# A fused attention and two-layer network kernel: weight conversion later in a double step, second-layer weights fetched in quarters, the last y stores on ScalarE's queue, two pools moved

## The chip, the cores and the metric

The kernel runs on one core of a Trainium2 chip. The metric is the device time of one execution in microseconds. Before the change three runs took 1278.15, 1279.85 and 1282.69 us, median 1279.85 us.

## The reference

```
o = softmax(q k^T / 8) v            # 8 batches x 8 heads, in 9 chunks of 64 rows, head size 64
x = o as [4608 tokens, 512]
h = x @ w_in                        # 512 -> 1024
s = h * softmax(h);  z = (s - mean) / sqrt(var + 1e-6) * g_ln
y = z @ w_out                       # 1024 -> 512
h2 = y @ w_in2                      # 512 -> 2048
out = (max(h2, 0) + alpha * min(h2, 0)) @ w_out2      # 2048 -> 512
```

All inputs arrive as 64-bit floats and the result is 32-bit. Each product of the two networks is built from three matmuls on operands split into a high and a low part. The weights are converted to such pairs on the chip.

## The kernel before, in words

All instructions are issued in the order in which the program writes them. Each engine works through its own list, and waits where an operand or a buffer is not free yet.

**Phase 1** (to about 567 us) takes 36 tiles of 128 tokens through attention, the first network and its normalisation. The first ten tiles follow a written list. From tile 10 each turn of a loop, called a step here, emits the entries of STEP for step i; an entry `name+d` means operation `name` of tile i+d. The ones that matter below: `hm` (L456, L462) multiplies x by w_in; `sq` (L492) squares; `xh` and `xl` (L442, L447) split the next x; `zv` (L497) makes the variance; `pw` (L503, on GpSimd) takes its power -1/2; `zs` (L507, VectorE) scales by it; `qs` and `qn` (L395, L402, VectorE) sum and normalise the attention weights of a later tile; `tr` (L409, TensorE) transposes these, right behind `hm`.

Beside this, `conv` converts one unit of weights: ScalarE takes the top bits apart (L142, L143), VectorE makes the low part (L154 `g`, L157 `f`), GpSimd makes the sign (L148) and the sum (L342). In front of that it runs what is due for the second network's weights: sums of two blocks on GpSimd (L220), a split in high (`hi`, L229, ScalarE) and low (`lo`, L230, GpSimd), and the stores of both to DRAM. Every step has one `conv`. The steps in `twice` have a second one; such a step is called a double step here. There are three: 20, 24 and 28.

The list LAST ends phase 1: it stores the last results y (`ysb`, two stores of 128 KB each, ystore, L565 and L569) and begins phase 2's first loads.

**Phase 2** (about 567 to 926 us) computes the first product of the second network, with seven products where a plain two by two block scheme has eight. Tokens are taken in six groups of 768 (s), features in eight blocks (b): 48 units. A unit has 42 matmuls in seven products, p1, p6, p5, p7, p2, p3, p4, into four PSUM banks `hx`, `hy`, `hz`, `hv`; p2, p3 and p4 add to banks that p1, p5 and p7 filled, after the first value of the bank has been read. ScalarE and VectorE turn the banks into four results `g`, stored by SyncE as `gd` (192 KB each). There are six `g` buffers, and a buffer is written again only when its store has landed. The weights of one block, W[b], are 1792 KB. W[0] and W[1] are loaded during LAST, W[2] and W[3] behind LAST, and W[4] to W[7] one each in the units 0 to 3 (load_w, L686). In the last token group each W[b] is replaced by the output weights of the same number, behind unit b (L691).

**Phase 3** computes the last product from `gd` and these weights, with operands named `f..` and `r..`.

SBUF pools grow from a left and a right end. Phase 2's pools lie on those of phase 1, and a tile there waits until the tile of phase 1 under it has been used for the last time. From the right end the order of phase 1 is `e`, `s`, `sm`, `zt` (the tile `zz`, read by the last matmuls of phase 1), `wo1`, `y`; that of phase 2 is a small tile, then the weights W[2], W[7], W[3], W[6], W[5], W[4], then the `g` buffers.

Of the kernel before, what the change touches and what calls it, by code (L numbers as in the profile page):

```python
# [9 lines left out]
F32 = mybir.dt.float32  # L10
F32R = mybir.dt.float32r
# [19 lines left out]
YT = 4  # L31
YG = 128 * YT
YP = 256
SG = 384
NS = NT // (2 * SG)
PAIRS = NT // 2
NB2 = KF2 // 2
# [5 lines left out]
def order(text):  # L43

    return [(m[1], int(m[2])) for m in re.finditer(r"([a-zA-Z]+)([-+]?\d+)", text)]
# [23 lines left out]
STEP = order(  # L69
    """  # L70
    q+3 v+3 ye-6 zh-2 zl-2 conv+0 hm+0 tr+1 te+1 qk+2 hx+0 he+0 qm+2 qe+2 pv+1 zt-1 so+0 sq+0
    ya-5 conv+1 xh+1 xl+1 zv+0 pw+0 qs+2 zs+0 qn+2 yb-5 yx-5
    """
)
CONV = order(
    """
    p+0 l-1 s+0 a-1 f+2
# [15 lines left out]
def tile_chunk_attention_solu_prelu(  # L93
# [12 lines left out]
    nc = tc.nc  # L106
# [11 lines left out]
    y_dram = [dram.tile([128, K1, 2 * SG], F32, name=f"yd{j}") for j in range(NS)]  # L118
# [3 lines left out]
    wi_dram = dram.tile([128, NB2, 2, 7, 2, 128], F32, name="wid")  # L122
    wo_dram = dram.tile([128, NB2, 2, 7, 256], F32, name="wod")
# [44 lines left out]
    def phase1():  # L168
        with ExitStack() as c1, ExitStack() as c0:
            L = lambda name, bufs, **k: c0.enter_context(tc.tile_pool(name=name, bufs=bufs, side="left", **k))  # L170
            R = lambda name, bufs, **k: c1.enter_context(tc.tile_pool(name=name, bufs=bufs, side="right", **k))
# [6 lines left out]
            ep = R("e", 1)  # L178
            sp = R("s", 2)
            sm = R("sm", 2)  # L180
            ztp = R("zt", 1)
            wop = R("wo1", 1)
            yp = R("y", 2)
# [5 lines left out]
            qs, vs = {}, {}  # L189
# [15 lines left out]
            for kk in range(K1):  # L205
                for n in range(2):
                    c = slice(512 * n, 512 * n + 512)
# [4 lines left out]
            raws, tops, parts, his = {}, {}, {}, {}  # L212
# [117 lines left out]
            def unit_sign(u, eng):  # L330
                tops[u] = conv_sign(stage, *tops[u], eng)
# [28 lines left out]
            def unit_lo(u, eng):  # L360
                f, hi = parts.pop(u), his.pop(u)
                eng.tensor_tensor(out=units[u][2] if u < UI else wo["l"][:, u - UI], in0=f, in1=hi.bitcast(F32), op=ALU.subtract)  # L362
# [200 lines left out]
            def ystore(j, m):  # L563
                y = yp.tile([128, YG], F32, name="ysb", tag="ysb")
                nc.scalar.activation(out=y, in_=ypend.pop((j, m)), func=AF.Copy)  # L565
                pairs = (0, 1) if Z_SLOTS[j][0][0] < Z_SLOTS[j][1][0] else (1, 0)
                for c, p in enumerate(pairs):
                    g, o = divmod(j * YG + p * YP, 2 * SG)
                    nc.sync.dma_start(out=y_dram[g][:, m, o:o + YP], in_=y[:, c * YP:(c + 1) * YP])  # L569

            def yevac(s):
                assert ("yb", s) in done
# [4 lines left out]
            def yfirst(s):  # L577
# [10 lines left out]
                q=load_q, v=load_v, f=fetch, p=unit_top, l=unit_low, h=unit_hi,  # L588
                s=lambda u: unit_sign(u, nc.gpsimd), S=lambda u: unit_sign(u, nc.vector),
                a=lambda u: unit_add(u, nc.gpsimd), A=lambda u: unit_add(u, nc.vector),  # L590
                o=lambda u: unit_lo(u, nc.gpsimd), O=lambda u: unit_lo(u, nc.vector),
# [3 lines left out]
                g=lambda _: nc.sync.dma_start(out=g_sb, in_=g_ln.rearrange("(k p) -> p k", p=128)),  # L595
# [24 lines left out]
            for name, i in FIRST:  # L620
                if name in "ho" and i >= UO:
                    run_post(next(u for u in range(len(units)) if ("a", u) not in done) + 1)
                else:
                    emit(name, i)
            twice = {20, 24, 28}
            k = 0
            while ("p", k) in done:
                k += 1
            for i in range(FIRST_TILES, TILES):
                for name, d in STEP:  # L630
                    if name == "conv":
                        if d == 0 or i in twice:
                            run_post(k)
                            for c, e in CONV:
                                emit(c, k + e)
# [33 lines left out]
    def phase2():  # L669
        with ExitStack() as c2:  # L670
            def P(name, bufs, side="left", stack=c2, **k):
                return stack.enter_context(tc.tile_pool(name=name, bufs=bufs, side=side, reuse_waits="tile", **k))

            NL = 2
            wl = P("w2l", 1)
            ps2 = [P("ps_2l", 1, space=PSUM)]
            ca = c2.enter_context(ExitStack())
            tp = [P(f"t2{i}", 1, stack=ca) for i in range(26)]
            up = P("u2", 1, stack=ca)
            wr = {}  # L680
            W, raw, th, tl = {}, {}, {}, {}

            def load_w(b, src):
                W[b] = (wr.get(b) or wl).tile([128, 2, 7, 256], F32R, name=f"w2{b}", tag=f"w{b}")
                if src is wi_dram:
                    nc.sync.dma_start(  # L686
                        out=W[b].bitcast(F32).rearrange("p t i c -> p (t i c)"),
                        in_=src[:, b].rearrange("p t i k c -> p (t i k c)"),
                    )
                else:  # L690
                    nc.sync.dma_start(out=W[b].bitcast(F32), in_=src[:, b])  # L691

# [9 lines left out]
            def free(t):  # L704
                slots.append(homes.pop(t.name))

            def load_y(s):
                at[0] = s % 2 == 0
                for t in ("11", "12", "22", "21"):
                    r, c = int(t[0]) - 1, int(t[1]) - 1  # L710
                    raw[t] = slot(F32 if t == "12" else F32R, f"y{t}", at[0])
                    nc.sync.dma_start(
                        out=raw[t].bitcast(F32), in_=y_dram[s][:, 2 * r:2 * r + 2, SG * c:SG * c + SG]
                    )
# [134 lines left out]
            for b in range(NL):  # L849
                load_w(b, wi_dram)  # L850
# [12 lines left out]
                wr[b] = P(f"w2r{b}", 1, side="right")  # L863
            ps2.append(P("ps_2r", 1, side="right", space=PSUM))
            gp = P("g2", 1, side="right", stack=ca)
            for b in range(NL, NL + 2):
                load_w(b, wi_dram)

# [4 lines left out]
            src, t4s, ops, ops0 = {}, {}, {}, {}  # L875
# [154 lines left out]

            early = {(4, 1): "p1", (5, 1): "p6", (6, 1): "p5", (6, 2): "p7", (7, 1): "p2", (7, 2): "p3", (7, 3): "p4"}
            sums = {(2, 0): 0, (2, 3): 1, (3, 0): 2, (4, 0): 3}
            prev, first = None, []
            for s in range(NS):
                for b in range(NB2):
                    def extra(k):
                        if s == 0 and k == 1 and NL + 2 + b < NB2:
                            load_w(NL + 2 + b, wi_dram)
                        if s + 1 == NS:
                            if (b, k) == (0, 3):  # L1040
                                load_g(pieces[0])
                            if (b, k) == (6, 5):
                                load_g(pieces[1])
                            if b in (3, 4, 5, 6) and k in (2, 3):
                                if (b, k) == (3, 2):
                                    first.append(first_piece(pieces[0]))
                                next(first[0])
                        else:
                            if (b, k) == (1, 0):
                                load_y(s + 1)  # L1050
                            if (b, k) in sums:
                                sum_y(sums[b, k])
                            if (b, k) in early:
                                high_y(s + 1, early[b, k])
                            if (b, k - 1) in early:
                                low_y(s + 1, early[b, k - 1])

                    prev = unit(s * NB2 + b, s, b, prev, extra)
                    if s + 1 == NS and b < 7:
                        load_w(b, wo_dram)  # L1060
            for k in range(3):
                prev.late(k)
            for t, p in enumerate(GROUPS[0]):
# [27 lines left out]
    with tc.manual_schedule():  # L1091
        phase1()
# [32 lines left out]
```

## Time and profile before

| | |
|---|---|
| median of three runs | 1279.85 us |
| the profiled execution | 1281.57 us, its span 1279.7 us |
| busy share of the span | TensorE 97%, its weight loads 87%, VectorE 73%, ScalarE 53%, GpSimd 26% |
| mean granted TensorE clock | 0.990 of full speed |

TensorE has something to do nearly all the time, so time can be gained only where it waits. In the profile the time of an instruction is counted from the span's start. Behind an instruction, `[us <-X]` is the idle time of its engine in front of it and what ended it. SPq is SyncE's queue of transfers. PE is TensorE, DVE VectorE, ACT ScalarE, POOL GpSimd. In a matmul's row the time is from its start to its modelled end; neighbours overlap.

### The profile page before, as it was taken

Reading aid. Unit: us, or ns where it says so; the run is one execution under the profiler, and the core shown is the slowest. Engines: PE = TensorE matmul, PEld = TensorE weight load, DVE = VectorE, ACT = ScalarE, POOL = GpSimd, SP = SyncE. Lnnn points to the kernel's source line nnn. Section 1 sums busy time; section 2 is a strip of 40 time slices with the busy share of each in tenths; the row PEclk is TensorE's granted clock in tenths of the full one; section 3 lists DMA queues with packets and bytes.
Section 4 is the critical chain, followed back from the end, with each engine's and each line's share of the span. In section 5 each row is a group of like instructions: output and inputs, shape, how many; then the busy total and the mean of one; then the engine's idle time right before and its main releaser. Section 6 shows DMA issues by size and latency. Waiting matters only on the chain. (4 is left out here: it accounts for less than half of the span.)

```text
span 1279.7 us, 21741 instructions
## 1 busy us (share of the span) xinstructions
PE 1236.0 (97%) x8160; PEld 1108.6 (87%) x8160; DVE 933.9 (73%) x1423; ACT 682.4 (53%) x1140; POOL 326.6 (26%) x309
## 2 busy tenths in 40 slices
PE   6789999999999899998999999999999999999998
PEld 5678888888888788888999999999989888888898
DVE  6985587777877677434878787777876959678684
ACT  6685455556555555434666676665644344344442
POOL 4664155535565644412020202200000000000000
PEclk9889999999999999998999999999999999999999
DMA  8453356554656552549343443428996638374462
GB/s 323 154 150 110 104 170 186 172 183 154 229 188 229 177 180 75 201 157 380 139 157 116 151 158 114 155 111 302 338 341 207 223 119 295 97 264 148 159 220 99
DMA packets 145225, 237.88 MB, mean 186 GB/s; under 512 B 14432, under 2 KB 99936, under 8 KB 143072
## 3 DMA queue, kind: packets, MB, share of 16 engines
q1 hardware_dynamic: 144960, 235.71, 53.7%
q8 instruction: 64, 1.05, 0.3%
q0 software_dynamic: 160, 0.79, 0.1%
q14 instruction: 41, 0.34, 0.1%
HBM read 149.68 MB, written 86.77 MB: 185 GB/s over the span
## 5 line engine op out<-in xcount | busy, mean ns | idle before, releaser
L789 DVE SCALAR_TENSOR_TENSOR g<-ng,nal,g 128x384 f32<-128x384 f32 x192 | 123.7, 644 | 50.4 <-ACT g L667 50.4
L667 ACT ACTIVATE ng<-g 128x384 f32<-128x384 f32 x144 | 75.8, 526 | 128.1 <-DVE g L661 128.1
L750 PE MATMUL hx<-th,w 128*128 128x384 f32 x384 | 113.8, 337 | 5.1 <-ACT s L667 5.1
L164 PE MATMUL yps<-zz,wo_h 128*128 128x512 f32 x288 | 115.2, 400 | 0.0
L750 PE MATMUL hv<-th,w 128*128 128x384 f32 x384 | 113.6, 336 | 0.4 <-DVE g L661 0.4
L750 PE MATMUL hz<-th,w 128*128 128x384 f32 x384 | 113.7, 336 | 0.3 <-DVE wv L661 0.3
L166 PE MATMUL yps<-zz,wo_l 128*128 128x512 f32 x288 | 112.4, 390 | 0.0
L165 PE MATMUL yps<-zz,wo_h 128*128 128x512 f32 x288 | 112.2, 390 | 0.0
L983 PE MATMUL oz<-rhi,w 128*128 128x512 f32 (+1 forms) x304 | 93.8, 369 | 0.6 <-DVE osb L661 0.6
L983 PE MATMUL ox<-rhi,w 128*128 128x512 f32 (+1 forms) x304 | 93.8, 369 | 0.0
L983 PE MATMUL ov<-rhi,w 128*128 128x512 f32 (+1 forms) x304 | 93.7, 369 | 0.0
L664 POOL TENSOR_TENSOR yt<-y,y 128x384 f32<-128x384 f32 x24 | 26.9, 1140 | 240.0 <-DMA y<-yd 240.0
L667 ACT ACTIVATE rhi<-rt 128x1024 fp32r<-128x1024 f32 (+1 forms) x56 | 54.6, 984 | 61.7 <-DVE rt L664 16.3
L667 ACT ACTIVATE g<-g 128x384 f32<-128x384 f32 x144 | 75.2, 522 | 3.1
L750 PEld LDWEIGHTS hx<-th,w 128*128 128x128 f32 x384 | 71.3, 189 | 5.8 <-ACT s L667 5.8
L664 DVE TENSOR_TENSOR rlo<-rt,rhi 128x1024 fp32r<-128x1024 f32 (+1 forms) x56 | 62.5, 1126 | 15.4 <-ACT rhi L667 15.1
L750 PEld LDWEIGHTS hv<-th,w 128*128 128x128 f32 x384 | 71.3, 189 | 0.9 <-DVE g L661 0.9
L750 PEld LDWEIGHTS hz<-th,w 128*128 128x128 f32 x384 | 71.3, 189 | 0.6 <-DVE wv L661 0.6
L456 PE MATMUL h<-wi_h,xh 128*128 128x512 f32 x256 | 69.3, 393 | 0.0
L456 PE MATMUL h<-wi_l,xh 128*128 128x512 f32 x256 | 68.8, 390 | 0.2 <-POOL wi_l L362 0.2
L492 ACT ACTIVATE eh<-sl,st 128x1024 f32<-128x1024 f32 x36 | 41.5, 1152 | 45.0 <-DVE st L487 45.0
L750 PE MATMUL hx<-y,w 128*128 128x384 f32 x192 | 64.5, 336 | 0.0
(179 smaller groups left out, 3268.6 us busy)
## 6 DMA issues: line engine op xcount, KB each, us to landing
gd<-g SPq DMA_DIRECT2D x192, 192.0 KB, 1.8
qkt<-in_qk SPq DMA_DIRECT2D x36, 512.0 KB, 5.3
w<-wid SPq DMA_DIRECT2D x8, 1792.0 KB, 10.9
w<-wod SPq DMA_DIRECT2D x8, 1792.0 KB, 10.1
rc<-gd SPq DMA_DIRECT2D x24, 512.0 KB, 3.9
rd<-gd SPq DMA_DIRECT2D x24, 512.0 KB, 4.9
raw<-in_moe_w_out SPq DMA_DIRECT2D x24, 511.8 KB, 4.4
vt<-in_v SPq DMA_DIRECT2D x36, 256.0 KB, 4.4
```

The lines of the kernel that those rows point to most:

```text
L164: nc.tensor.matmul(o, lh, rh, start=first, stop=False)
L165: nc.tensor.matmul(o, lh, rl, start=False, stop=False)
L166: nc.tensor.matmul(o, ll, rh, start=False, stop=last)
L456: nc.tensor.matmul(ps[:, n], xh[:, kk], w[:, kk, 512 * n:512 * n + 512], start=(kk == 0 and w is wi_h), stop=False,)
L492: nc.scalar.activation(out=e, in_=s, func=AF.Square, bias=st[:, 4:5], accum_out=st[:, 5:6])
L664: eng.tensor_tensor(out=out, in0=a, in1=b, op=ALU.subtract)
L667: nc.scalar.activation(out=out, in_=in_, func=func, **k)
L750: nc.tensor.matmul(self.ps[x], w[:, a, i, k], d[:, k], start=(p not in CHAINED and k + j == 0), stop=(k == 1 and j == 2), skip_group_check ...
L789: nc.vector.scalar_tensor_tensor(out=self.g[t], in0=self.n[t], scalar=nal_sb[:, f:f + 1], in1=self.g[t], op0=ALU.mult, op1=ALU.add)
L983: nc.tensor.matmul(bank[key, m][:, :n], W[2 * j + k][:, a, i, 128 * m:128 * m + 128], d[:, k], start=(p not in CHAINED and j + k + q == 0) ...
```

## The change

1. The steps with a second conversion are 20, 26 and 31 in place of 20, 24 and 28. The second one now stands behind `pw`, where it stood in front of `xh`.
2. A pool of 2 KB per partition, never used, stands between `sm` and `zt`. The small phase 2 pool `u2` moves from the left end to the right, behind the `g` buffers.
3. The y stores of the last two groups of four tiles are issued by ScalarE.
4. Behind LAST only W[2] is loaded. The blocks W[3] to W[7] are loaded in four quarters of 448 KB each during the units 0 to 4, at places 0, 2, 3 and 5 of the seven places of a unit, so one block per unit and three units ahead of its use. The output weights of block b are loaded in the same way during unit b+1.
5. The four loads of the next token group's y stand at four places of unit 1 in place of one.

```diff
-    ya-5 conv+1 xh+1 xl+1 zv+0 pw+0 qs+2 zs+0 qn+2 yb-5 yx-5
+    ya-5 xh+1 xl+1 zv+0 pw+0 conv+1 qs+2 zs+0 qn+2 yb-5 yx-5
+TWICE = {20, 26, 31}
...
             sm = R("sm", 2)
+            R("pad", 1).tile([128, 512], F32, name="pad")
...
-                    nc.sync.dma_start(out=y_dram[g][:, m, o:o + YP], in_=y[:, c * YP:(c + 1) * YP])
+                    (nc.sync if j < YT + 3 else nc.scalar).dma_start(
...
-            up = P("u2", 1, stack=ca)
...
-            for b in range(NL, NL + 2):
-                load_w(b, wi_dram)
+            up = P("u2", 1, side="right", stack=ca)
+            load_w(NL, wi_dram)
...
+                c = slice(0, 3584) if q is None else slice(896 * q, 896 * q + 896)
+                nc.sync.dma_start(out=to[:, c], in_=of[:, c])
...
+            parts = (0, 2, 3, 5)
...
-                        if s == 0 and k == 1 and NL + 2 + b < NB2:
-                            load_w(NL + 2 + b, wi_dram)
+                        if s == 0 and k in parts and NL + 1 + b < NB2:
+                            load_w(NL + 1 + b, wi_dram, parts.index(k))
+                        if s + 1 == NS and b and k in parts:
+                            load_w(b - 1, wo_dram, parts.index(k))
...
-                            if (b, k) == (1, 0):
-                                load_y(s + 1)
+                            if b == 1 and k < 4:
+                                load_y(s + 1, YQ[k:k + 1])
...
-                    if s + 1 == NS and b < 7:
-                        load_w(b, wo_dram)
```

**GpSimd in step 20**, a double step before and after. `st<-st,mhalf` is `pw`; `lo`, `a` (the sign) and `f` (the sum) are the two conversions. Before:

```order
L148 TENSOR_TENSOR a_3439<-pos,neg 128x512
L342 TENSOR_TENSOR f_3436<-f_3436,a_3277 128x512
L230 TENSOR_TENSOR lo<-f_3436,hi 128x512
L230 TENSOR_TENSOR lo<-f_2953,hi 128x512
L148 TENSOR_TENSOR a_3566<-pos,neg 128x512
L342 TENSOR_TENSOR f_3563<-f_3563,a_3439 128x512
L503 TENSOR_TENSOR st<-st,mhalf 128x1
```

And with the change:

```order
L149 TENSOR_TENSOR a_3443<-pos,neg 128x512
L344 TENSOR_TENSOR f_3440<-f_3440,a_3281 128x512
L505 TENSOR_TENSOR st<-st,mhalf 128x1
L232 TENSOR_TENSOR lo<-f_3440,hi 128x512
L232 TENSOR_TENSOR lo<-f_2957,hi 128x512
L149 TENSOR_TENSOR a_3576<-pos,neg 128x512
L344 TENSOR_TENSOR f_3573<-f_3573,a_3443 128x512
```

`pw` moved ahead of the four operations of the second conversion; in the lists of ScalarE and VectorE `xh`, `xl` and `zv` moved ahead of it in the same way, and VectorE's `g` and `f` stand between `zv` and `qs`.

**SyncE's queue at the start of phase 2**, with what each transfer waits for: DMAHW0 to DMAHW7 are eight counters that the transfers use in turn, so such a wait is mostly one for the landing of the transfer eight places back. `w` is a block of weights, `yd<-ysb` a y store, `y<-yd` a y load. Before:

```order
L569 DMA yd_70<-ysb 128x256 [waits DMAHW6_49,Activation_49]
L569 DMA yd_70<-ysb 128x256 [waits DMAHW7_49]
L686 DMA w_6338<-wid 128x3584 [waits DVE_49,DMAHW0_49,PE_49,Pool_49]
L686 DMA w_6340<-wid 128x3584 [waits DMAHW1_49]
L686 DMA w_6362<-wid 128x3584 [waits DMAHW2_49]
L794 DMA gd_76<-g 128x384 [waits DMAHW3_49,DVE_49]
L794 DMA gd_73<-g 128x384 [waits DMAHW4_49,DVE_49]
L712 DMA y_6432<-yd_66 128x2x384 [waits DMAHW5_49]
```

And with the change, from W[1] (`w_6103`) on; `w_6343` is W[2], `w_6357` W[3]:

```order
L692 DMA w_6103<-wid 128x3584 [waits DMAHW3_49,DVE_49,PE_49]
L692 DMA w_6343<-wid 128x3584 [waits DVE_49,DMAHW0_49,PE_49,Activation_49]
L692 DMA w_6357<-wid 128x896 [waits DMAHW7_49,DVE_49,PE_49]
L692 DMA w_6357<-wid 128x896 [waits DMAHW2_49]
L692 DMA w_6357<-wid 128x896 [waits DMAHW3_49]
L797 DMA gd_76<-g 128x384 [waits DMAHW4_49,DVE_49]
L797 DMA gd_73<-g 128x384 [waits DMAHW5_49,DVE_49]
L692 DMA w_6357<-wid 128x896 [waits DMAHW6_49]
L692 DMA w_6438<-wid 128x896 [waits DMAHW7_49]
L715 DMA y_6440<-yd_66 128x2x384 [waits DMAHW0_49]
```

In front of the first `gd` store three whole blocks became one block, which follows W[1] directly, and three quarters.

**ScalarE at the same place**: `ysb` is the evacuation of the last y result, `s<-hx` the first of phase 2. Before:

```order
L667 ACTIVATE th<-y_6096 128x768 [waits DMAHW2_49,DMAHW0_49]
L565 ACTIVATE ysb<-yps 128x512 [waits DMAHW1_49,DMAHW0_49,PE_49]
L667 ACTIVATE th<-yt_6182 128x768
L565 ACTIVATE ysb<-yps 128x512 [waits DMAHW3_49,DMAHW2_49,PE_49]
L667 ACTIVATE s_6352<-hx 128x384 [waits PE_49]
```

And with the change:

```order
L671 ACTIVATE th<-yt_6183 128x768
L567 ACTIVATE ysb<-yps 128x512 [waits DMAHW4_49,DMAHW3_49,PE_49]
L571 DMA yd_70<-ysb 128x256 [waits DMAHW0_49,Activation_49]
L571 DMA yd_70<-ysb 128x256
L671 ACTIVATE s_6355<-hx 128x384 [waits PE_49]
```

In all sixteen stores moved into ScalarE's list, and one of the last two also waits for a counter, DMAHW0, that belongs to the transfer of W[2].

## Rows read from the trace of the kernel before

**Rows 1.** The page, part 1: TensorE's busy time, share, instructions; then other engines.

```profile
PE   1236.0 (97%) x8160; PEld 1108.6 (87%) x8160; DVE 933.9 (73%) x1423; ACT 682.4 (53%) x1140; POOL 326.6 (26%) x309
```

**Rows 2.** Timeline, the transposes `tr`: start us, us, engine, line, operation, count, [idle before].

```profile
309.40 0.60 PE L409 MATMUL et<-ident,e 128*128 128x128 f32 x4
325.20 0.63 PE L409 MATMUL et<-ident,e 128*128 128x128 f32 x4 [0.90 <-DVE e L402]
...
412.08 0.60 PE L409 MATMUL et<-ident,e 128*128 128x128 f32 x4
426.47 0.60 PE L409 MATMUL et<-ident,e 128*128 128x128 f32 x4
444.56 0.63 PE L409 MATMUL et<-ident,e 128*128 128x128 f32 x4 [3.46 <-DVE e L402]
...
460.51 0.60 PE L409 MATMUL et<-ident,e 128*128 128x128 f32 x4
```

**Rows 3.** Timeline of double step 28: `pw`, `zs`, `qn`.

```profile
440.43 0.55 POOL L503 TENSOR_TENSOR st<-st,mhalf 128x1 f32<-128x1 f32 x1
...
441.01 1.75 DVE L507 TENSOR_SCALAR sl<-sl,st 128x1024 f32<-128x1024 f32 x1 [3.86 <-POOL st L503]
...
442.68 1.74 DVE L402 TENSOR_TENSOR e<-e,r 128x512 f32<-128x512 f32 x1
```

**Rows 4.** Timeline of the regular step 31: `zs`, `qn` and the `tr` behind them.

```profile
483.38 0.76 DVE L507 TENSOR_SCALAR sl<-sl,st 128x1024 f32<-128x1024 f32 x1
...
484.06 0.69 DVE L402 TENSOR_TENSOR e<-e,r 128x512 f32<-128x512 f32 x1
...
489.30 0.60 PE L409 MATMUL et<-ident,e 128*128 128x128 f32 x4
```

**Rows 5.** Timeline, VectorE's part of a conversion while GpSimd works.

```profile
501.13 0.86 DVE L154 TENSOR_SCALAR g<-a 128x512 uint16<-128x512 uint16 x1
...
502.03 1.66 DVE L157 SCALAR_TENSOR_TENSOR f<-raw,g 128x512 f32<-128x512 uint32 x1
```

**Rows 6.** Timeline, the first matmul of p6 in units 0, 1 and 4.

```profile
568.33 0.33 PE L750 MATMUL hy<-th,w 128*128 128x384 f32 x1
...
575.61 0.33 PE L750 MATMUL hy<-th,w 128*128 128x384 f32 x1
...
606.30 0.33 PE L750 MATMUL hy<-th,w 128*128 128x384 f32 x1
```

**Rows 7.** Timeline, the weight transfers at the start of phase 2 and the stall.

```profile
569.05 1.29 SPq L686 DMA_DIRECT2D w<-wid  x3
...
587.85 0.56 DVE L661 TENSOR_TENSOR g<-hz,u 128x384 f32<-128x384 f32 x1 [6.60 <-DMA gd<-g]
...
590.39 0.69 PE L750 MATMUL hx<-th,w 128*128 128x384 f32 x1 [4.22 <-ACT s L667]
```

**Rows 8.** Windows: stretch, length, engines' busy time, granted clock, DMA share, GB/s.

```profile
10.00:12.00 2.00, 1.12 (x12) 0.91 (x8) 1.97 (x4) 1.01 (x2) 1.14 (x2) 1.00 1.03 412
...
542.00:544.00 2.00, 2.00 (x14) 1.78 (x14) 0.00 (x0) 1.06 (x2) 2.00 (x3) 1.00 1.01 430
...
558.00:560.00 2.00, 2.00 (x10) 1.66 (x9) 1.03 (x2) 1.06 (x2) 0.00 (x0) 1.00 0.38 131
```

**Rows 9.** DMA issues, 558 to 560 us: transfer, issuer, count, size, us to landing.

```profile
yd<-ysb SPq DMA_DIRECT2D x1, 128.0 KB, 1.8
```

**Rows 10.** Timeline, the last y evacuation and the first `g` of unit 0.

```profile
567.46 0.60 ACT L565 ACTIVATE ysb<-yps 128x512 f32<-128x512 f32 x1 [1.39 <-PE yps L166]
...
571.65 0.56 DVE L661 TENSOR_TENSOR g<-hv,wv 128x384 f32<-128x384 f32 x1 [0.48 <-PE hv L750]
```

**Rows 11.** Timeline, the first matmul of p6 in units 46 and 47.

```profile
912.06 0.33 PE L750 MATMUL hy<-th,w 128*128 128x384 f32 x1
...
920.06 0.33 PE L750 MATMUL hy<-th,w 128*128 128x384 f32 x1
```

**Rows 12.** Chain of work that ended last, in the same stretch: start us, us, what.

```profile
905.88 11.23 DMA gd<-g
```

More of the change, by code (lines that the diff above doesn't have):

```diff
@@ L568, in ystore @@
                     g, o = divmod(j * YG + p * YP, 2 * SG)
-                    nc.sync.dma_start(out=y_dram[g][:, m, o:o + YP], in_=y[:, c * YP:(c + 1) * YP])
+                    (nc.sync if j < YT + 3 else nc.scalar).dma_start(
+                        out=y_dram[g][:, m, o:o + YP], in_=y[:, c * YP:(c + 1) * YP]
+                    )
             def yevac(s):
@@ L624, in phase1 @@
                     emit(name, i)
-            twice = {20, 24, 28}
+            twice = TWICE
             k = 0
@@ L678, in phase2, with load_w @@
             tp = [P(f"t2{i}", 1, stack=ca) for i in range(26)]
-            up = P("u2", 1, stack=ca)
             wr = {}
             W, raw, th, tl = {}, {}, {}, {}
[L683 to L691, printed above, removed]
+            def load_w(b, src, q=None):
+                if not q:
+                    W[b] = (wr.get(b) or wl).tile([128, 2, 7, 256], F32R, name=f"w2{b}", tag=f"w{b}")
+                to = W[b].bitcast(F32).rearrange("p t i c -> p (t i c)")
+                of = src[:, b].rearrange("p t i k c -> p (t i k c)" if src is wi_dram else "p t i c -> p (t i c)")
+                c = slice(0, 3584) if q is None else slice(896 * q, 896 * q + 896)
+                nc.sync.dma_start(out=to[:, c], in_=of[:, c])
             slots = list(range(26))
@@ L705, in free, with load_y @@
                 slots.append(homes.pop(t.name))
-            def load_y(s):
+            YQ = ("11", "12", "22", "21")
+            def load_y(s, which=YQ):
                 at[0] = s % 2 == 0
-                for t in ("11", "12", "22", "21"):
+                for t in which:
                     r, c = int(t[0]) - 1, int(t[1]) - 1
```

## The prediction

> **What bounds the kernel now.** Read first the busy shares: TensorE is at work 97% of the span [rows 1], so the change can win only where TensorE waits, and the next question is where. The list of TensorE's waits names the lines, and the timeline of these lines gives the price of each, by comparing distances between equal points of the program rather than adding idle times: what follows a wait runs slower for a while too (the first matmul after the long stall takes 0.69 us instead of 0.33 [rows 7, 6]), and a distance has both.
>
> In phase 1 the transposes come every 14.39 us in regular steps (412.08 to 426.47 [rows 2]). Around step 28 the two distances are 18.09 and 15.95 us, 5.26 more than two regular ones; around step 20 one is 15.80, 1.41 more [rows 2]. That is 6.67 us lost in double steps; the third, 24, cost less and is left out. The cause: in step 28 `pw` runs only at 440.43, behind both conversions in GpSimd's list; VectorE had stood idle 3.86 us for it, then needed 1.75 and 1.74 us for `zs` and `qn` [rows 3], and the transposes waited 3.46 us [rows 2].
>
> In phase 2 a unit takes 7.28 us (568.33 to 575.61). Unit 4 should have come 29.12 us after unit 0, but came after 37.97 [rows 6]: 8.85 us lost. Three whole blocks of weights, 5.5 MB, are issued at 569.05; the first stores of results stand behind them, a result waits 6.60 us for its buffer, and TensorE 4.22 us for the bank [rows 7].
>
> At the end of phase 2 unit 47 came 8.00 us after unit 46 [rows 11], 0.72 too late, in a stretch where a store took 11.23 us to land [rows 12]. The rest of phase 3 is a row of matmuls that the change doesn't touch.
>
> **Double steps.** Nothing is added or removed: a second conversion is moved in three steps. `pw` no longer stands behind it, so it follows `zv` at once, as in a regular step. There `qn` ends at 484.75 and `tr` starts at 489.30 [rows 4]: 4.55 us to spare. What is late next is VectorE: `g` and `f` now stand between `zv` and `qs`, and GpSimd's half of the second conversion now runs beside `zs` and `qn`. Beside GpSimd `g` and `f` take 0.86 and 1.66 us [rows 5], `zs` 1.75 in place of 0.76 and `qn` 1.74 in place of 0.69 [rows 3, 4]: in all 2.52 + 0.99 + 1.05 = 4.56 us at most, just the spare time. So the stall goes, with nothing to spare; for what is handed on to the next step (its first reduction starts late) I take 0.3 us per double step, between 0 and 1.0 (the lengthening of one slowed VectorE operation). This gives 6.67 - 0.9 = 5.8 us gained, with ends of 3.7 and 7.1 (step 24 as well).
>
> The Trainium skill says why the slowed operations must be counted: "SBUF — State Buffer", section "Who interferes with whom", has VectorE and GpSimd share one pair of ports under an exclusive lock, held for a whole instruction, by operations with two inputs in SBUF too. The trace agrees: 1.74 against 0.69 us for `qn`. Without this rule one would expect three double steps free of any loss; with it they just fit.
>
> **The start of phase 2.** With the pad W[2] no longer lies on `zz`, and it follows W[1] directly in SyncE's queue, since the twelve y stores between them are gone; these two loads fall into LAST, where the transfers have room (a share of 0.38 at 558 us [rows 8]). W[3] still lies on `zz` and starts at the end of phase 1, but only three quarters of it, 1.38 MB instead of 5.5 MB, precede the first result stores. At 426 GB/s (430 at a share of 1.01 [rows 8]) that is 3.2 us, over before unit 0's first stores at about 574 us. In the 7.3 us behind, four stores, four quarters and four y loads pass, 0.79 + 1.84 + 1.57 = 4.2 MB or 9.9 us: transfers fall some 2.6 us behind. A result buffer is written again about one unit, 7.28 us, after its result is stored; 2.6 plus 1.8 for landing [rows 9] leaves 2.9 us. So the wait of 6.60 us goes. I leave 0.75 us as lost, with ends of 0 and 2.6 (if the backlog shows in full): 8.85 - 0.75 = 8.1 gained, from 6.2 to 8.85.
>
> New there: the last two y stores are issued by ScalarE in front of `s`. The trace shows no transfer issued by ScalarE; the nearest row is SyncE's, 1.29 us for three, 0.43 each [rows 7], taken whole; the other end is none. The evacuation ends at 568.06 [rows 10], so `s` starts at 568.9 and ends half a microsecond later. p2, the first product that needs it, comes three products of 1.04 us after 568.33, at 571.45: nothing waits. The first `g` now lies where the last y was and waits for its stores. Issued by 568.9 they land at 570.7, and `g` starts at 571.65 [rows 10]; even 2 us later, since they share the engines with W[3], `g` would end at 573.3, before p4 at 573.53. Price nothing; the other fourteen stores fall where ScalarE is half idle (53% busy [rows 1]). Pad and `u2` move addresses only. The loads of y at four places, in the five later token groups, come at most 3.5 us later and are needed a unit later: nothing either.
>
> **The end of phase 2.** Seven blocks of 1.835 MB now travel as quarters, with rows of 3.5 KB instead of 14 KB. The nearest row is of 512 KB loads with 4 KB rows, 412 GB/s at a share of 1.03, so 400; the whole blocks had 426, and stores with rows of 1 KB 131 at 0.38, so 345 [rows 8]. A block takes 4.31 us at 426, 4.59 at 400, 5.32 at 345: 0.28 more each, 2.0 for seven; at the far end 7.1. The transfers are the limit of this stretch, so I count it whole. Against it stands the 0.72 us of unit 47: a store now queues behind one quarter, not a block. Net loss 1.3, from a gain of 0.7 to a loss of 7.1.
>
> The Trainium skill speaks against the quarters: "DMA: Bandwidth & Descriptors", section "Bandwidth", asks for transfers of at least 1 MiB to reach 75% of the peak. The row of 512 KB loads at 400 GB/s, with several under way at once, does not bear it out; were it to hold, the loss would be like the far end's.
>
> **Sum.** -5.8 - 8.1 + 1.3 = -12.6 us. The profiled execution took 1281.57 us, 1.72 more than the median; so 1269.0 for such an execution and 1267.2 against the median 1279.85.
>
> **Rivals.**
> 1. *The double steps keep their loss.* VectorE's slowed operations use up the spare time exactly; if the next step starts late each time, or steps 26 and 31 meet GpSimd's longer conversions, the 5.8 is not gained: -6.8, 1273.0. For it: no reserve. Against: step 20 ran `pw` three conversions late and lost only 1.41.
> 2. *Quarters travel slowly.* At 345 GB/s the end loses 7.1 - 0.7 = 6.4: -7.5, 1272.4. For it: rows of 3.5 KB are shorter; against: the 4 KB rows. The skill's rule on 1 MiB would act here.
> 3. *ScalarE is held.* One of the last two y stores waits for W[2]. If W[2] still had to wait for `zz`, it would land near 567.7 + 4.3 + 1.8 = 573.8, `s` would end at 574.4, and p2 would wait 3 us, some 4.5 with the slow matmuls behind (3.46 us of waiting cost 5.26 at step 28): -8.1, 1271.8. Against: W[2] ends where the pad ends.
> 4. *Slower: eight transfers under way.* A transfer waits for the one eight places back, and with quarters a unit has just eight. So in units 41 to 47 no unit can be shorter than a transfer's way from issue to landing. With 7.28 us or less that costs nothing; at the 11.23 us of [rows 12] it is 3.95 us for each of seven units, 27.7: +13.8 (without the 1.3), 1293.7. It decides from 7.28 + 13.9 / 7 = 9.3 us on. For it: that row. Against: it stood behind a whole block, and a backlog of eight is 1.84 + 0.79 = 2.6 MB, 6.6 us at 400 GB/s.
>
> **How the numbers follow.** The forecast has 0.73, the rivals 0.10, 0.05, 0.06 and 0.06. A measurement of this kernel tells 0.3%, 3.8 us, from no change. The forecast's own range is from 1263 (all losses gone, the end even) to 1272; with the first three rivals and some allowance for two at once it reaches 1275, and below 1260, where the waits at phase 3's start would have to go too, I expect nothing. Rivals 1 to 3 are faster as well; faster 0.90, within 0.3% 0.05 (two rivals together), slower 0.05, nearly all of it rival 4.
>
> **What would show it.** Transposes every 14.4 us through steps 20, 26 and 31, with `pw` right behind `zv`. The first matmuls of p6 in units 0 to 4 at 7.28 us, no wait of a `g` for its store, W[2] issued near 543 us. ScalarE's last y stores short, with `s` less than 1 us late. In the last token group units near 7.3 us, and stores landing in under 7 us. A new TensorE wait at steps 27 or 32, or units of 8 us in the last group, would make it wrong.

## The result, and the profile after

The changed kernel takes 1267.98 us (median of 5 runs, 1267.67 to 1268.12), the kernel before 1279.80 in the runs beside it; the ratio is 0.9906, with an interval from 0.9891 to 0.9920. The prediction was 1267.2. The profiled execution of the changed kernel took 1267.81 us (span 1265.8).

**Phase 1.** The timeline around step 26, now a double one: transposes (L411), `pw` (L505), `zs` (L509), `qn` (L404), and what is left of a stall.

```profile
393.74 0.60 PE L411 MATMUL et<-ident,e 128*128 128x128 f32 x4
...
401.34 0.55 POOL L505 TENSOR_TENSOR st<-st,mhalf 128x1 f32<-128x1 f32 x1 [3.11 <-DVE st L499]
...
403.52 1.62 DVE L509 TENSOR_SCALAR sl<-sl,st 128x1024 f32<-128x1024 f32 x1
...
404.55 1.62 POOL L149 TENSOR_TENSOR a<-pos,neg 128x512 bf16<-128x512 bf16 x1
...
405.07 1.65 DVE L404 TENSOR_TENSOR e<-e,r 128x512 f32<-128x512 f32 x1
...
406.13 1.62 POOL L344 TENSOR_TENSOR f<-f,a 128x512 f32<-128x512 f32 x1
...
407.78 0.63 ACT L231 ACTIVATE hi<-f 128x512 fp32r<-128x512 f32 x1 [3.38 <-POOL f L344]
...
408.14 0.60 PE L411 MATMUL et<-ident,e 128*128 128x128 f32 x4
...
409.93 0.57 ACT L416 ACTIVATE ets<-et 128x512 f32<-128x512 f32 x1
...
410.56 1.15 PE L432 MATMUL xd<-ets,vt 64*64 64x64 f32 x32 [0.75 <-ACT ets L416]
...
423.49 0.60 PE L411 MATMUL et<-ident,e 128*128 128x128 f32 x4
```

The transpose behind the double step comes in time (14.40 us), since `pw` now waits only for VectorE's `zv`, and `qn` ends 1.42 us ahead of it; in [rows 2, 3] the transpose had to wait for `qn`. But the distance after it is 15.35. The first copy of step 27's conversion, `hi<-f`, reads a sum that GpSimd finishes at 407.75, as the last work of the second conversion of step 26; ScalarE waits 3.38 us for it, evacuates the transposes late, and `xd` waits 0.75. The same happens in step 32 (15.36); behind step 20 nothing does (14.39, 14.45). Over all steps, 5.2 us are gained of the 6.67 of [rows 2, 3].

**The end of phase 1 and the start of phase 2**, timeline: W[2], the y stores on ScalarE's queue (ACTq), and unit 0 (`hy` is the first product of p6).

```profile
535.19 0.32 SPq L692 DMA_DIRECT2D w<-wid  x1
...
536.70 0.81 ACTq L571 DMA_DIRECT2D yd<-ysb  x2
...
547.46 0.60 ACT L567 ACTIVATE ysb<-yps 128x512 f32<-128x512 f32 x1 [7.22 <-DMA yd<-ysb]
...
552.26 0.50 PE L165 MATMUL yps<-zz,wo_h 128*128 128x512 f32 x1 [0.79 <-ACT ysb L567]
...
560.75 1.27 SPq L692 DMA_DIRECT2D w<-wid  x3
...
561.39 0.81 ACTq L571 DMA_DIRECT2D yd<-ysb  x2
561.62 0.33 PE L753 MATMUL hy<-th,w 128*128 128x384 f32 x1
...
562.25 0.49 ACT L671 ACTIVATE s<-hx 128x384 f32<-128x384 f32 x1 [0.89 <-PE hx L753]
...
567.87 0.56 DVE L665 TENSOR_TENSOR g<-hv,wv 128x384 f32<-128x384 f32 x1 [3.42 <-DMA yd<-ysb]
...
568.49 0.44 PE L753 MATMUL hv<-th,w 128*128 128x384 f32 x1 [1.50 <-DVE g L665]
...
570.70 0.33 PE L753 MATMUL hy<-th,w 128*128 128x384 f32 x1
...
585.26 0.33 PE L753 MATMUL hy<-th,w 128*128 128x384 f32 x1
...
592.93 0.33 PE L753 MATMUL hy<-th,w 128*128 128x384 f32 x1
```

The waits of 6.60 and 4.22 us in [rows 7] are gone. Unit 4 comes 31.31 us after unit 0, against 37.97 in [rows 6]; the 2.19 us still lost are 1.80 in unit 0 and 0.39 in unit 3. In unit 0 the first `g` waits for the last y stores, which lie where it writes. The DMA issues show why. The last pair, 561 to 562 us:

```profile
yd<-ysb ACTq DMA_DIRECT2D x2, 128.0 KB, 5.3
```

A store that landed in 1.8 us in [rows 9] needs 5.3 (4.7 and 5.9 for the two) among three quarters of W[3], the first of them issued 0.6 us ahead on the other queue. Behind W[1] and W[2] it is worse; the first store of the pair at 536.70 (issues from 535 to 537 us):

```profile
yd<-ysb ACTq DMA_DIRECT2D x1, 128.0 KB, 9.7
```

For this pair ScalarE waits 7.22 us, and hands 0.79 to TensorE. W[1], issued at 528.48, took 13.2 us to land, until 541.65. So W[2], issued at 535.19, went out where the transfers were full (windows, columns as in [rows 8]):

```profile
535.00:541.60 6.60, 6.60 (x32) 5.44 (x31) 2.18 (x2) 2.96 (x4) 5.50 (x7) 1.00 1.00 423
541.60:547.00 5.40, 5.40 (x26) 4.46 (x24) 0.00 (x0) 0.00 (x0) 0.00 (x0) 1.00 0.92 351
```

**What a wait costs beyond itself.** The third number from the end of a windows row is TensorE's granted clock. Two stretches of the kernel before, behind its waits of 3.46 us [rows 2] and 4.22 us [rows 7], and one of the changed kernel, behind its 1.50 us in unit 0:

```profile
444.50:449.00 4.50, 4.43 (x72) 4.18 (x73) 4.43 (x7) 1.83 (x4) 2.09 (x2) 0.65 0.58 198
590.40:594.00 3.60, 3.60 (x11) 3.60 (x12) 2.08 (x4) 0.72 (x2) 2.51 (x3) 0.50 1.06 447
568.50:571.00 2.50, 2.50 (x14) 2.50 (x15) 1.35 (x3) 2.00 (x5) 0.00 (x0) 1.00 0.04 10
```

With the long waits the clock fell, from 590.40 on to 0.50 of full speed, which is 1.2 GHz in place of 2.4; behind the 1.50 us it stayed at 1.00. So removing those two waits gained more than their own length; the distances contain both.

**The end of phase 2.** Unit 47 comes 7.28 us after unit 46 (8.00 in [rows 11]):

```profile
898.69 0.33 PE L753 MATMUL hy<-th,w 128*128 128x384 f32 x1
...
905.97 0.33 PE L753 MATMUL hy<-th,w 128*128 128x384 f32 x1
```

But the first wait of the last phase is longer. TensorE's waits from 905 to 940 us (line, releaser, us in all, times, longest):

```profile
PE ox L986 <- DVE ra L668: 2.4, 1, 2.4
```

The same wait in the kernel before:

```profile
PE ox L983 <- DVE ra L664: 1.6, 1, 1.6
```

From unit 47 to the last product 355.22 us pass, 0.86 more than before.

### The profile page after: what moved, and what is told of

It reads as the page before. It is cut to its first block, busy times and chain, and to the rows that moved or that the text cites. A ratio compares the mean times of both kernels' runs of the same rounds, so it can differ in the third digit from the quotient of the medians.

```text
span 1265.8 us, 21771 instructions
## 1 busy us (share of the span) xinstructions
PE 1227.7 (97%) x8160; PEld 1102.9 (87%) x8160; DVE 935.3 (74%) x1423; ACT 682.5 (54%) x1140; POOL 327.9 (26%) x309
## 3 DMA queue, kind: packets, MB, share of 16 engines
q8 instruction: 64, 1.05, 0.3%
## 4 chain that ended last, share of the span: by engine, by line
PE 47%; DMA 5%; DVE 1%; issue 0%; SPq 0%; ACT 0%; DVEq 0%; ACTq 0%
PE oz L986 7%; PE ov L986 7%; PE ox L986 7%; PE hz L753 7%; PE hv L753 6%; PE hx L753 6%; PE oy L986 3%; PE hy L753 3%; DMA w<-wod 3%; DMA rc<-gd 1%; DMA gd<-g 0%; DVE rt L668 0%; DVE rb L668 0%; DVE rlo L668 0%; DVE u L665 0%
## 5 line engine op out<-in xcount | busy, mean ns | idle before, releaser
L167 PEld LDWEIGHTS yps<-zz,wo_l 128*128 128x128 f32 x288 | 54.0, 188 | 11.7
```

Of the source, the lines that this page charges most:

```text
L167: nc.tensor.matmul(o, ll, rh, start=False, stop=last)
```

## The experiments

Every kernel was timed in 5 rounds beside the kernel before. All distances below are read from the timelines: "steps" from the transpose near 138 us to the last of phase 1; "LAST" from there to `hy` of unit 0; "start" what ten units from unit 0 on take beyond 72.8 us; "end" from `hy` of unit 47 to the last product. The ratio is to the kernel before, with its interval.

| kernel | us | ratio | steps | LAST | start | end |
|---|---|---|---|---|---|---|
| before | 1279.8 | | 378.01 | 50.24 | 8.85 | 354.36 |
| changed | 1267.98 | .9906 (.9891-.9920) | 372.80 | 50.81 | 2.19 | 355.22 |
| e1 steps only | 1274.45 | .9962 (.9951-.9974) | 372.79 | 50.25 | 8.88 | 354.11 |
| e2 without steps | 1273.25 | .9955 (.9944-.9967) | 378.00 | 51.05 | 1.78 | 354.87 |
| e3 doubles 20, 25, 30 | 1268.11 | .9913 (.9900-.9926) | 372.93 | 51.18 | 1.56 | 354.98 |
| e10 doubles 20, 24, 28 | 1269.09 | .9925 (.9911-.9940) | 372.80 | 50.88 | 1.84 | 354.92 |
| e5 y on SyncE | 1269.29 | .9927 (.9916-.9939) | 372.73 | 50.26 | 4.23 | 355.82 |
| e4 ng on y | 1267.17 | .9911 (.9896-.9926) | 372.73 | 50.99 | 1.05 | 353.84 |
| e6 W[3..7] whole | 1271.88 | .9947 (.9934-.9959) | 372.83 | 51.03 | 5.01 | 354.84 |
| e7 no pad | 1265.32 | .9894 (.9881-.9908) | 372.73 | 49.71 | 1.62 | 355.16 |
| e8 last weights whole | 1266.80 | .9915 (.9899-.9931) | 372.79 | 51.15 | 2.11 | 353.40 |
| e13 doubles 12, 15, 18, ng | 1266.15 | .9900 (.9884-.9916) | 371.19 | 51.24 | 1.13 | 354.35 |
| e15 no pad, early, late y | 1265.75 | .9901 (.9888-.9915) | 371.16 | 49.71 | 2.55 | 356.26 |
| e17 no pad, early, whole | 1264.15 | .9884 (.9867-.9900) | 371.15 | 49.71 | 2.10 | 354.49 |

"Steps" repeats to 0.1 us where the steps are the same. The times scatter by 1 to 3 us, much of it ahead of these distances: the transpose near 138 us starts between 137.2 and 138.9 in the other profiles and at 140.08 in that of before, whatever was edited. So effects under 2 us are read from the table's distances, not from the medians.

**Do the two halves add?** e1 is the kernel before with the new `STEP` and the new double steps:

```diff
-    ya-5 conv+1 xh+1 xl+1 zv+0 pw+0 qs+2 zs+0 qn+2 yb-5 yx-5
+    ya-5 xh+1 xl+1 zv+0 pw+0 conv+1 qs+2 zs+0 qn+2 yb-5 yx-5
-            twice = {20, 24, 28}
+            twice = {20, 26, 31}
```

> The kernel before with the new place of the conversion and the new double steps 20, 26, 31, and nothing else of the change. Theory: the double steps are worth what the two traces differ by between the transposes of tile 13 and tile 35, 338.23 - 333.02 = 5.2 us, alone as in company: 1279.8 - 5.2 = 1274.6 us. Rival 1: they are worth less alone, because the stores of y and the load of W[2] stay as before and the late second conversion of step 31 runs into them: 1276 to 1278. Rival 2: the 2.07 us by which the changed kernel is ahead already at the transpose of tile 10 belong to these edits too: 1272.5, and that transpose starts near 138.0 us, not near 140.1.

e2 is the changed kernel with these two edits undone.

> The changed kernel with the conversion back in its old place and the double steps back at 20, 24, 28: what is left is quarters, ScalarE's queue and the shift by 2 KB. Theory (the two halves add): 1268.0 + 5.2 = 1273.2 us, with unit 0 of phase 2 at 9.1 us between its hy products as in the changed kernel. Rival 1 (they do not add, part of the gain of phase 2's start comes from a phase 1 that ends with less work in its queues): 1274.5 or more, and the wait of the first g longer than 3.4 us. Rival 2 (the 2.07 us ahead of the first transpose come from the shift of the pools): 1271 to 1272, and the transpose of tile 10 near 138.0 us.

Measured: 1274.45 and 1273.25; by the ratios 0.38% and 0.45%, together 0.83%, against 0.94% for both at once, which the intervals allow. Each stage has its gain with its own edits alone (5.22 in "steps" for e1; 7.07 in "start" for e2). Rival 2 of both expectations fell: the transpose of tile 10 is early in both, at 138.56 in e1 and 138.05 in e2, and the two share no edit, so nothing here ties the 2 us ahead of it to a half.

**What makes the step behind a double one late?** Three kernels move the double steps (`TWICE`), one of them (e10) back to the old numbers with the conversion in its new place.

```diff
-TWICE = {20, 26, 31}
+TWICE = {20, 25, 30}   (e3)
+TWICE = {20, 24, 28}   (e10)
+TWICE = {12, 15, 18}   (e13, with ng as in e4)
```

> The changed kernel with the double steps at 20, 25, 30 in place of 20, 26, 31, so that the first conversion of each double step has an even number. Theory: the four sums of a pair of w_out2 rows belong to the odd conversions and their halves are read by the next, even, conversion. In steps 26 and 31 both stand in one step, and ScalarE's copy waits 3.4 us for GpSimd's sums; with an even one first the sums have a whole step before they are read. Both steps of 15.35 us shrink to about 14.4: 1268.0 - 1.9 = 1266.1 us. Rival 1: any second conversion that late costs this, whatever its number: 1268.0 within 0.5. Rival 2: the four sums on GpSimd (about 3 us) now stand behind the first conversion's work in the double step itself and hold the next step's low parts longer: 1269 to 1270.

> The changed kernel with the conversion in its new place in the step, but the double steps at 20, 24, 28 as before. Theory: the place makes the whole gain (pw no longer stands behind the second conversion on GpSimd), the numbers of the double steps nothing: step 20 loses nothing, the steps behind 24 and 28 take 15.35 us each since the conversion there reads what GpSimd makes in the one before, as behind 26 and 31. 1268.0 within 0.4. Rival: doubles at 24 and 28 lie closer and the second meets a backlog: step 28 or 29 loses 1.5 us or more, 1269.5.

e3's theory fell and its rival 1 gave the time: the steps behind 25 and 30 take 15.40 and 15.42 us. e10 loses the same behind 24 and 28 (15.37, 15.38), and nothing in step 20; "steps" is 372.80, that of the changed kernel. So the place of the conversion makes the whole gain, and the choice of steps none of it. The theory that was left: the first copy of a conversion always reads what GpSimd makes in the conversion ahead of it, except at numbers that leave 2 when divided by 4 in the w_in2 part. The step behind step 20 has such a number, 34.

> The changed kernel with two edits: ng on y's space as in the run with ng tiles apart, and the double steps at 12, 15, 18. Theory: a step behind a double one is late (15.35 instead of 14.39) because the first copy of its conversion reads what GpSimd makes in the second conversion of the double step; this holds for every conversion number except those that leave 2 when divided by 4 in the part that converts w_in2, whose first copy reads a sum made a step before (this is why the changed kernel loses nothing behind step 20, and why even numbers did not help: 15.40 twice). Steps 13, 16 and 19 are such, so all three double steps cost nothing: -1.9, with unit 0's 1.8: 1268.0 - 3.7 = 1264.3 us. Rival 1: the knock-on comes from GpSimd's load in any double step, here in all three: 1267. Rival 2: the conversions of w_in2 have more sums on GpSimd and more stores than those of w_out2, and early steps pay for them: 1268 or more.

The transposes behind the double steps 12, 15 and 18 in e13, from its timeline:

```profile
207.00 0.60 PE L411 MATMUL et<-ident,e 128*128 128x128 f32 x4
...
250.18 0.60 PE L411 MATMUL et<-ident,e 128*128 128x128 f32 x4
...
264.90 0.60 PE L411 MATMUL et<-ident,e 128*128 128x128 f32 x4
...
293.69 0.60 PE L411 MATMUL et<-ident,e 128*128 128x128 f32 x4
```

Only one distance is long (250.18 to 264.90, 14.72 us, behind step 15); behind step 12, from 207.00 on, and behind step 18, from 293.69 on, none is over 14.43. "Steps" falls by 1.6 us to 371.19, and repeats in e15 and e17. That agrees with the theory but for the 0.33, whose cause stays open (TensorE shows no wait there). The exception itself is read from the program: all three steps behind have a number that leaves 2, and no run puts a double step in front of another number of the w_in2 part, so "any early step" is a rival left untested. The time, 1266.15 (1264.35 to 1267.98), is too scattered to show it alone.

**The y stores and the first `g`.**

```diff
-                    (nc.sync if j < YT + 3 else nc.scalar).dma_start(   (e5)
+                    nc.sync.dma_start(
+            np_ = P("n2", 1, side="right", stack=ca)     (e4, between gp and up)
-                self.n[t] = self.tile("ng", gp, 2)
+                self.n[t] = self.tile("ng", np_, 2)
```

> The changed kernel with every store of y back on the SP queue, the rest kept. W[2] now stands behind the last stores in that queue. Theory: unit 0's 1.8 us and the 0.57 us at the end of phase 1 come from stores of y that travel beside loads of W issued ahead of them on another queue (5.9 us to land where 1.8 is usual); in one queue the stores go first and W follows: first g waits for nothing, 1268.0 - 2.4 = 1265.6 us, if W[2], now issued near 561 us, lands before unit 2 at about 576. Rival 1: the stores wait behind W[0] and W[1], which SP issues only when phase 1 lets go of their space, and ScalarE's ysb waits for a buffer: 1268 to 1270. Rival 2: with W[2] and the quarters of W[3] behind each other, each unit at the start is paced by the loads, as before: about 1.5 us in each of units 2 to 4, 1270 to 1272.

> The changed kernel with the two ng tiles of phase 2 in a pool of their own between g and u2, so that it is they, and no longer the first two g, that lie where the last y tile was. The stores of y stay on ScalarE's queue and land as late as before. Theory: TensorE's 1.5 us in unit 0 come only from the first g waiting for those stores; now ScalarE's first ng waits for them (to about 567.8 us), for which nothing on TensorE is due within a unit. Unit 0 takes 7.3 us instead of 9.1: 1268.0 - 1.8 = 1266.2 us. Rival: ScalarE, held 1.5 to 2 us, hands the wait on, s of unit 1 comes late and unit 1 or 2 loses what unit 0 gains: 1268.0 within 0.5.

In e5 the last pair lands in 1.8 us, although a whole block follows it in the queue (issues 559 to 561 us):

```profile
w<-wid SPq DMA_DIRECT2D x1, 1792.0 KB, 7.2
yd<-ysb SPq DMA_DIRECT2D x2, 128.0 KB, 1.8
```

Unit 0 takes 7.28 us and LAST is back at 50.26: both losses come from stores that travel behind loads. But W[2] now goes out last, together with W[3], the next y and the first results, and unit 3 loses 4.23 us (rival 2, in one unit instead of three): TensorE waits 2.2 us, and from 588 to 592 us its granted clock is 0.57. In sum e5 is no better: 1269.29.

e4 leaves the stores late and moves who waits for them:

```profile
565.67 0.56 DVE L665 TENSOR_TENSOR g<-hv,wv 128x384 f32<-128x384 f32 x1 [0.48 <-PE hv L753]
...
568.20 0.52 ACT L671 ACTIVATE ng<-g 128x384 f32<-128x384 f32 x1 [4.73 <-DMA yd<-ysb]
```

Now ScalarE waits 4.73 us, unit 0 takes 7.28, and units 1 and 3 lose 0.37 and 0.67, the rival in part: "start" goes from 2.19 to 1.05. Its time alone, 1267.17 (1265.79 to 1268.32), does not tell it from the changed kernel.

**Quarters and pad at the start.**

```diff
-                        if s == 0 and k in parts and NL + 1 + b < NB2:       (e6)
-                            load_w(NL + 1 + b, wi_dram, parts.index(k))
+                        if s == 0 and k == 1 and NL + 1 + b < NB2:
+                            load_w(NL + 1 + b, wi_dram)
-            R("pad", 1).tile([128, 512], F32, name="pad")                    (e7)
```

> The changed kernel with W[3] to W[7] loaded whole (1.8 MB in one transfer, during the unit ahead, behind its p6) instead of in quarters; W[2], the shift of the pools, ScalarE's queue and the loads for the last phase as changed. Theory: the quarters matter because the stores of g and the loads of y stand between them; behind a whole block they wait some 4.5 us more, g tiles come free late, and units 1 to 4 lose about 1 us each: 1271 to 1273 us. Rival: the size of the pieces is worth nothing, the gain at the start of phase 2 comes from the unit by which each load is put off and from W[2] being early: 1268.0 within 0.6.

> The changed kernel without the 2 KB that shift the pools: W[2] again lies on the first 2 KB of zz and can be loaded only when phase 1's last products have read it, near 560 us instead of 535. Theory: W[2], the quarters of W[3], the last stores of y, y of the next slice and the first stores of g then share 15 us, as in the kernel before, and half of the 6.7 us come back, with the waits on g in units 1 to 3: 1271 to 1272 us. Rival 1: 15 us are enough for W[2] and W[3] (3.6 MB at the 412 GB/s of the trace are 9 us), and the end of phase 1 loses the 0.57 us that W[2] costs it now: 1267 to 1268. Rival 2: W[2] isn't there at unit 2 and the whole 6.7 come back: 1274.7.

e6 has the time that the theory gave, 1271.88, but not by its mechanism. 4.02 of its 5.01 us are lost in unit 0:

```profile
569.75 0.56 DVE L665 TENSOR_TENSOR g<-hv,wv 128x384 f32<-128x384 f32 x1 [4.12 <-DMA yd<-ysb]
570.37 0.69 PE L753 MATMUL hv<-th,w 128*128 128x384 f32 x1 [2.20 <-DVE g L665]
```

The stores and the clock behind the wait:

```profile
yd<-ysb ACTq DMA_DIRECT2D x2, 128.0 KB, 6.6
...
570.40:573.70 3.30, 3.30 (x10) 3.30 (x11) 2.08 (x4) 2.77 (x7) 0.00 (x0) 0.50 0.19 67
```

The last y stores need 6.6 us behind a whole W[3], 5.3 among its quarters, and TensorE waits 2.20 us instead of 1.50. Unit 0 loses 2.22 us more than in the changed kernel: 0.70 is the longer wait, the other 1.52 the matmuls behind it, which run at half the clock here and at full clock there. So at the start the pieces matter because the last y stores get through sooner between smaller ones; the stores of results, which the theory named, cost less than 1 us.

e7 came out on the other side of its theory: without the pad the kernel is faster, 1265.32 (1265.14 to 1265.79), by more than rival 1 said; by the distances it is 1.8 us ahead of the changed kernel. Rival 1 has the mechanism, as far as the end of phase 1 goes. Its timeline:

```profile
537.81 0.83 ACTq L570 DMA_DIRECT2D yd<-ysb  x2
...
542.62 0.60 ACT L566 ACTIVATE ysb<-yps 128x512 f32<-128x512 f32 x1 [3.09 <-PE yps L167]
...
558.98 1.27 SPq L691 DMA_DIRECT2D w<-wid  x3
...
559.81 0.33 PE L752 MATMUL hy<-th,w 128*128 128x384 f32 x1
...
567.09 0.33 PE L752 MATMUL hy<-th,w 128*128 128x384 f32 x1
...
581.65 0.33 PE L752 MATMUL hy<-th,w 128*128 128x384 f32 x1
...
582.49 0.56 DVE L664 TENSOR_TENSOR g<-hz,u 128x384 f32<-128x384 f32 x1 [2.47 <-DMA gd<-g]
...
590.55 0.33 PE L752 MATMUL hy<-th,w 128*128 128x384 f32 x1
```

With W[2] out of the way until 559 us, `ysb` waits for its product and no longer for a store, and LAST is 1.10 us shorter (and 0.5 shorter than the 50.24 to 50.26 of before, e1 and e5, where the stores stand in SyncE's queue). Without the shift the first `g` lies on the y buffer ahead of the last, and unit 0 loses nothing. What is lost, 1.62 us, is lost in unit 3, where the transfers are full (window 560 to 590 us; the last three numbers are the clock, the DMA share and GB/s):

```profile
560.00:590.00 30.00, 28.95 (x165) 28.31 (x164) 18.03 (x32) 14.66 (x32) 8.75 (x8) 1.00 1.02 390
```

**Quarters at the end.** e8 loads the last phase's weights whole, as before:

```diff
-                        if s + 1 == NS and b and k in parts:
-                            load_w(b - 1, wo_dram, parts.index(k))
+                    if s + 1 == NS and b < 7:     (behind the unit)
+                        load_w(b, wo_dram)
```

> The changed kernel with the weights of the last phase loaded whole again, one block of 1.8 MB at the end of each unit of the last token group, as in the kernel before; W[2] to W[7] stay in quarters. Theory: the quarters cost nothing there and take away the 0.72 us of unit 47, so without them unit 47 takes 8.00 us again: 1268.0 + 0.7 = 1268.7 us. Rival 1 (the prediction's term): the transfers pace that stretch and 3.5 KB rows are slower, so whole blocks gain 2.0 and lose 0.7: 1266.7. Rival 2: more than the units is at stake, the first steps of the last phase wait for blocks that come later: 1270 or more.

Unit 47 comes after 7.28 us here too (and in e1, which also has whole blocks): whole blocks alone do not bring the 0.72 us back, so the theory fell. What made unit 47 late in the one profile of the kernel before stays open. The first wait of the last phase is shorter, in e8's waits from 905 to 940 us:

```profile
PE ox L986 <- DVE ra L668: 0.8, 1, 0.8
```

"End" is 353.40, and over all kernels 353.4 to 354.5 with whole blocks (4 kernels) and 353.8 to 356.3 with quarters (10): the means differ by 0.9, so the quarters cost about 1 us, though the ranges overlap. This is the direction of rival 1. By ratio e8 (0.9915) can't be told from the changed kernel (0.9906).

**Put together.** e15 takes e7, the early double steps, and loads the second group's y one unit later; e17 takes e7, the early double steps and e8's whole blocks.

```diff
-                            if b == 1 and k < 4:                (e15)
+                            if b == 1 + (s == 0) and k < 4:
```

> A version put together from the runs: the changed kernel without the 2 KB, the double steps at 12, 15, 18, and the loads of y for the second token group one unit later (during unit 2 instead of 1), its four sums at (3,2), (4,0), (4,3), (5,0) of unit and product. Theory: from 1265.3 without the shift, 1.6 go with the double steps (0.33 us lost instead of 1.92), and the 1.62 us that unit 3 still loses go at least by half, since 1.57 MB of y no longer travel between 568 and 580 us, where g waits 2.47 us for its store: 1262.1 to 1263.7 us. Rival 1: the engines of the transfers are full from 560 to 592 us whatever the order, and unit 4 or 5 loses what unit 3 gains: 1263.7 to 1264.5. Rival 2: the sums of the next group come too late for its first units: 1265 or more.

> The changed kernel without the 2 KB, with the double steps at 12, 15, 18, and with the last phase's weights loaded whole at the end of the units, as before the change. Theory: the three gains seen one by one add: 1265.3 (without the shift) - 1.6 (0.33 us lost in double steps instead of 1.92) - 1.2 (first wait of the last phase 0.8 us instead of 2.2 to 2.4, TensorE from the last unit to its last product 1.2 to 1.8 us shorter) = 1262.5 us. Rival 1: the start of the last phase is paced by the transfers, and arriving there 1.6 us earlier only lengthens the first wait (2.9 us in the version with y put off): 1264. Rival 2: the unit after the fourth loses more, as in that version, where the stall moved to unit 4 and grew from 1.62 to 2.52 us: 1265.

In e15 the steps keep their gain, but unit 4 loses 2.52 us instead of unit 3's 1.62: rival 1, transfers that are full either way. Its time, 1265.75, is above what rival 1 gave, since "end" is the longest of all, which neither rival had named. e17 has the lowest time, 1264.15 (1262.87 to 1265.22, all below the changed kernel's runs). Against the changed kernel its four distances are shorter by 1.65, 1.10, 0.09 and 0.73, together 3.6 us; the medians differ by 3.8. Both rivals hold in part: unit 3 loses 2.10 instead of e7's 1.62, and "end" is 354.49, not e8's 353.40. The intervals of the two ratios still overlap (to 0.9900 and from 0.9891).

## Why the prediction was right

- **Double steps, -5.8: measured -5.2.** The stall went as described, `pw` right behind `zv`, and the transpose of the double step in time. The residual of 0.3 us a step was mis-sized: 0.05, 0.96 and 0.96. It was meant as VectorE starting late; the runs show ScalarE's first copy waiting for GpSimd's second conversion. That is the TensorE wait at steps 27 and 32 that the prediction named as what would make it wrong; it was there, but small.
- **Start of phase 2, -8.1: measured -6.7 there and +0.6 at the end of phase 1.** The waits on result stores went. The failing step is "Price nothing" for the y stores ahead of the first `g`: they were to land by 570.7, 1.8 us after their issue [rows 9], with 2 us allowed for W[3]. They needed 5.3 us, more than both together; `g` was held 3.42 us and unit 0 took 1.80 us longer. W[2] "where the transfers have room" was the second error: the share of 0.38 was read at 558 us, but W[2] was issued at 535.19 (the prediction expected 543), with the transfers full until 547, and the y stores behind it needed 9.1 to 10.3 us.
- **End of phase 2, +1.3: measured +0.1.** The quarters kept the pace, with units of 7.28 us. Their cost, about 1 us, shows in the first wait of the last phase, where I had not put it. The 0.72 us of unit 47 went, but they are also gone with whole blocks (e1, e8), so that term was not the quarters' gain.
- **The sum.** -12.6 predicted; the stages give -5.21 + 0.57 - 6.66 - 0.72 + 0.86 = -11.2, the medians -11.8. Against the forecast the double steps fell short by 0.6 us and the start of phase 2 by 2.0, and the end gave 1.2 back. That the total came within 1 us is in part luck: errors of both signs cancelled.
- **The rivals.** Rival 1 came true by a third: 1.9 of the 5.8 us stay lost, behind the double steps. Rival 2 fell: the end changed by 0.1 us in all and not by 6.4, and from 900 to 934 us the transfers moved 393 GB/s with quarters and 384 with e8's whole blocks; quarters of W[3] went at 408 (window below, 564 to 566 us, columns as in [rows 8]). Rival 4 fell too: units 41 to 47 come 7.28 us apart. Rival 3 named the right engine with the wrong cause: ScalarE is held not by its own issue behind W[2] but by an evacuation that waits for the store.

```profile
564.00:566.00 2.00, 2.00 (x14) 2.00 (x13) 0.46 (x1) 0.00 (x0) 0.00 (x0) 1.00 1.04 408
```

The Trainium skill's rule of 1 MiB ("DMA: Bandwidth & Descriptors", section "Bandwidth"), which spoke against the quarters, did not show as a rate: these transfers have 448 KB each.

## What to carry to other kernels

A second queue hardly helps a transfer past one that another queue has already sent (of the four stores behind W[2] one landed 0.65 us ahead of it, the others after it): put small stores that somebody waits for ahead of large loads, or let what lies on their buffer be needed late. When a double load of work is moved out of the critical step, look at the first reader of its last result in the step behind. Read whether a stretch is quiet where the load will be issued, not later in it: a load brought forward is worth only what the transfers already there don't lose; e7 shows that taking this part back was better.

## What the runs showed of the hardware

- A store of 128 KB landed in 1.8 us alone or ahead of a load, in 4.7 and 5.9 among three loads of 448 KB, and in 9.1 to 10.3 behind W[1] and W[2], loads of 1.8 MB, the first partly done, though these were issued on another engine's queue.
- TensorE's granted clock was 0.50 of full speed (1.2 GHz) for 3 us and more behind waits of 2.20 us (e6) and 4.22 us (before), and 1.00 behind one of 1.50 us (changed kernel).
- ScalarE's issue of two stores took 0.81 us, as long as SyncE's (0.80 in e5).
- The time ahead of the transpose near 138 us varies by 2.9 us between profiled executions of kernels with the same instructions up to there, while the later stages repeat to 0.1 us. What makes it vary was not tried.
